# The first V weights issued between the first two x tiles instead of behind both, and one hoisted statistics instruction put back

## The chip, the cores and the metric

The kernel runs on one core of a Trainium2 chip. The time is device microseconds of one execution; the "span" of a profile is the same execution without its launch, some 1.8 us shorter.

## The reference, cut to what matters

```python
x = A_x                                             # 2048 x 1024, bf16
h  = x + A(layernorm(x), wqkv, wo)                  # 32 heads of 32, causal, window of 256 keys
h2 = h + B(layernorm(h), w1, w2)                    # silu, 3584 wide
# A:  qkv = x @ wqkv ; softmax(q k^T) v ; @ wo
```

Only the beginning is touched here: the layernorm of the first 512 rows of x (four tiles of 128 rows), and V = layernorm(x) @ wqkv[:, 2048:3072].

## The kernel before: the parts that matter

All loads shown go through the queue of the Sync engine (SP). Ahead of everything, eleven dummy matmuls keep TensorE busy, so that its clock, which is granted at half or full speed, is up when the real work comes. Each x tile is normalised (VectorE, with a square root on ScalarE), transposed on TensorE, copied back by ScalarE, and then used by "V groups" of eight matmuls each.

```python
load_x(0, 0)                       # 256 KB
load_x(0, 1)
load_wqkv(2 * D)                   # V weights, columns 0..511: 1 MB, rows of 1 KB
load_wqkv(2 * D + 512)             # V weights, columns 512..1023
load_x(0, 2)
load_x(0, 3)
for c0 in (0, D, 512, D + 512):    # Q and K weights
    load_wqkv(c0)
...
for i in range(11):                # warming matmuls, on zeros
    nc.tensor.matmul(sc[0][:, i % 2, :], lhsT=warm[:, 0, 0:P], rhs=warm[:, 0, :], start=True, stop=True)
...
def ln_first(xt, st, rs, j, stats=None, then=None):
    ln_stats(xt, st, j, stats)                       # two bn_stats and a bn_aggr on VectorE
    nc.scalar.activation(out=rs[:, j:j + 1], in_=st[:, j, 1:2], func=ACT.Sqrt, bias=eps[:], scale=1.0)
    if then is not None:
        nc.vector.bn_stats(out=then[0], in_=then[1])  # half of the next tile's statistics
    nc.vector.reciprocal(out=rs[:, j:j + 1], in_=rs[:, j:j + 1])
    for h in range(2):
        ln_norm(xt[:, h * 512:(h + 1) * 512], st, rs, j)
...
stats1 = small.tile([P, 2, 6], F32, name="ln_st", tag="ln_st")
ln_first(x_ring[0], st, rs, 0, then=(stats1[:, 0, :], x_ring[1][:, 0:512]))
turn_first(x_ring[0], lnT_b[0], 0)                   # 8 transposes on PE, 2 copies on ACT
ln_first(x_ring[1], st, rs, 1, stats=stats1)
v_group(0, 0, 0, act)                                # 8 matmuls, tile 0 x first V weights
turn_first(x_ring[1], lnT_b[0], 1)
ln_first(x_ring[2], st, rs, 2)
v_group(0, 1, 0, act)                                # tile 1: the "second V group" below
v_group(0, 0, 1, act)
...
```

The softmax here doesn't subtract the row's maximum and nothing guards it: scores larger than these inputs give would overflow.

Of the kernel before, what the change touches and what calls it, by code (L numbers as in the profile page):

```python
# [9 lines left out]
F32 = mybir.dt.float32  # L10
# [4 lines left out]
P = 128  # L15
# [21 lines left out]
def kernel(  # L37
# [10 lines left out]
    nc = tc.nc  # L48
# [3 lines left out]
    S, D = x2d.shape  # L52
# [12 lines left out]
    small = ctx.enter_context(tc.tile_pool(name="small", bufs=2))  # L65
# [22 lines left out]
    def view(region, off, *dims):  # L88
        n = 1
        for d in dims:  # L90
            n *= d
        ap = region[:, off:off + n]
        if len(dims) == 2:
            return ap.rearrange("p (a b) -> p a b", b=dims[1])
        if len(dims) == 3:
            return ap.rearrange("p (a b c) -> p a b c", b=dims[1], c=dims[2])
        return ap
# [5 lines left out]
    x_ring = [view(r_o, i * 1024, 1024) for i in range(8)]  # L103
# [22 lines left out]
    def load_x(b, j):  # L126
        nc.sync.dma_start(out=x_ring[(b % 2) * 4 + j], in_=x2d[(b * 4 + j) * P:(b * 4 + j + 1) * P, :])  # L127

    def load_wqkv(c0):
        dst = wqk[:, :, c0:c0 + 512] if c0 < 2 * D else wv[:, :, c0 - 2 * D:c0 - 2 * D + 512]  # L130
        nc.sync.dma_start(out=dst, in_=wqkv_v[:, :, c0:c0 + 512])

    load_x(0, 0)
    load_x(0, 1)
    load_wqkv(2 * D)
    load_wqkv(2 * D + 512)
    load_x(0, 2)
    load_x(0, 3)
# [13 lines left out]
        nc.tensor.matmul(sc[0][:, i % 2, :], lhsT=warm[:, 0, 0:P], rhs=warm[:, 0, :], start=True, stop=True)  # L152


    def ln_stats(xt, st, j, stats=None):
        first = 0
        if stats is None:
            stats = small.tile([P, 2, 6], F32, name="ln_st", tag="ln_st")
        else:
            first = 1  # L160
        for c in range(first, 2):
            nc.vector.bn_stats(out=stats[:, c, :], in_=xt[:, c * 512:(c + 1) * 512])
        nc.vector.bn_aggr(out=st[:, j, :], in_=stats[:])

# [17 lines left out]
    def ln_norm(xt, st, rs, j):  # L182
        nc.vector.tensor_scalar(out=xt, in0=xt, scalar1=st[:, j, 0:1], scalar2=rs[:, j:j + 1],
                                op0=ALU.subtract, op1=ALU.mult)
# [1 line left out]
    def ln_transpose(xt, dst, j):  # L186
        nc.sync.dma_start_transpose(out=dst[:, :, j * P:(j + 1) * P], in_=xt)

    def ln_first(xt, st, rs, j, stats=None, then=None):
        ln_stats(xt, st, j, stats)  # L190
        nc.scalar.activation(out=rs[:, j:j + 1], in_=st[:, j, 1:2], func=ACT.Sqrt, bias=eps[:], scale=1.0)
        if then is not None:
            nc.vector.bn_stats(out=then[0], in_=then[1])
        nc.vector.reciprocal(out=rs[:, j:j + 1], in_=rs[:, j:j + 1])
        for h in range(2):
            ln_norm(xt[:, h * 512:(h + 1) * 512], st, rs, j)

    def turn_first(xt, dst, j):
        for h in range(2):
            for i in range(4):  # L200
                kt = h * 4 + i
                nc.tensor.transpose(out=tp_ps[h][:, i * P:(i + 1) * P], in_=xt[:, kt * P:(kt + 1) * P], identity=ident[:])  # L202
            nc.scalar.copy(out=dst[:, h * 4:(h + 1) * 4, j * P:(j + 1) * P],  # L203
                           in_=tp_ps[h][:, 0:512].rearrange("p (k q) -> p k q", q=P))

    def ln_tiles(tag):
        st = small.tile([P, 4, 2], F32, name=f"st_{tag}", tag=f"st_{tag}")
        rs = small.tile([P, 4], F32, name=f"rs_{tag}", tag=f"rs_{tag}")
        return st, rs
# [9 lines left out]
    def v_group(b, j, c, copy):  # L219
        acc = next_acc()  # L220
        for kt in range(KT):
            nc.tensor.matmul(acc, lhsT=lnT_b[b % 2][:, kt, j * P:(j + 1) * P], rhs=wv[:, kt, c * 512:(c + 1) * 512],  # L222
                             start=(kt == 0), stop=(kt == KT - 1))
        copy(out=v[:, b * 4 + j, c * 16:(c + 1) * 16, 0:DH], in_=acc.rearrange("p (h d) -> p h d", d=DH))  # L224
# [108 lines left out]


    st, rs = ln_tiles("a")
    stats1 = small.tile([P, 2, 6], F32, name="ln_st", tag="ln_st")
    ln_first(x_ring[0], st, rs, 0, then=(stats1[:, 0, :], x_ring[1][:, 0:512]))
    turn_first(x_ring[0], lnT_b[0], 0)
    ln_first(x_ring[1], st, rs, 1, stats=stats1)
    v_group(0, 0, 0, act)  # L340
    turn_first(x_ring[1], lnT_b[0], 1)
    ln_first(x_ring[2], st, rs, 2)
    v_group(0, 1, 0, act)
    v_group(0, 0, 1, act)
# [13 lines left out]
    def ln1_steps(b):  # L358
        st, rs = ln_tiles("a")
        xs = [x_ring[(b % 2) * 4 + j] for j in range(4)]  # L360
        steps = [lambda j=j: ln_stats(xs[j], st, j) for j in range(4)]
        steps += rstd_steps(st, rs)
        for j in range(4):
            steps.append(lambda j=j: ln_norm(xs[j], st, rs, j))
        return steps, [lambda j=j: ln_transpose(xs[j], lnT_b[b % 2], j) for j in range(4)]

    def ln2_steps(b):
        st, rs = ln_tiles("b")
        hb = h_blk[b]
        load = lambda: nc.sync.dma_start(out=hb, in_=h_dram[b * 512:(b + 1) * 512, :].rearrange("(j p) d -> p j d", p=P))  # L370
        steps = [load]
        steps += [lambda j=j: ln_stats(hb[:, j, :], st, j) for j in range(4)]
        steps += rstd_steps(st, rs)
        for j in range(4):
            steps.append(lambda j=j: ln_norm(hb[:, j, :], st, rs, j))
        turns = [lambda j=j: ln_transpose(hb[:, j, :], ln2T[b], j) for j in range(4)]
        return steps[:-2] + [turns[0], steps[-2], turns[1], steps[-1]] + turns[2:]
# [104 lines left out]
    for b in range(NB):  # L482
# [4 lines left out]
        for ft in range(FT):  # L487
# [8 lines left out]
            if b == 0 and 6 <= ft < 14:  # L496
                j, c = divmod(ft - 6, 2)
# [60 lines left out]
```

## Time and profile before

| | |
|---|---|
| time, median of 3 runs | 701.58 us (699.18 to 703.16) |
| span of the profiled run | 700.0 us |
| TensorE busy | 688.5 us, 98% of the span |
| first V weights: issued, landed | 1.73 us, 9.44 us |
| first and second V group start | 9.48 us, 13.04 us |

TensorE is the bound throughout; only the first 13 us hold waits that a reordered load could shorten. The lines for this stand in the prediction. A row gives the stretch, its length, the busy time and number of instructions of TensorE (PE), weight loads, VectorE, ScalarE and GpSimd, then TensorE's granted clock, the busy share of the 16 DMA engines, and what they moved in GB/s.

```profile
4.00:5.50 1.50, 1.50 (x5) 0.58 (x4) 1.47 (x5) 0.29 (x1) 0.00 (x0) 1.00 0.89 298
7.60:11.03 3.43, 1.55 (x7) 0.76 (x8) 0.90 (x3) 0.56 (x2) 0.00 (x0) 0.96 1.08 363
11.03:14.44 3.41, 3.10 (x15) 1.47 (x14) 1.29 (x2) 1.56 (x3) 0.00 (x0) 0.54 1.09 356
```

Read the last three columns. In the later two stretches, and in the full ones below, the DMA share is about 1.08 (above 1 where packets of one engine overlap); between 4.0 and 5.5 us it is 0.89 and 298 GB/s, though much was queued. And the clock falls. The stretches are those of the prediction; at the edges that the clock records of this trace have, in steps of 3.41 us, the fall is sharp:

```profile
7.31:10.73 3.42, 1.25 (x6) 0.68 (x7) 0.90 (x3) 0.85 (x3) 0.00 (x0) 1.00 1.08 361
10.73:14.14 3.41, 3.10 (x14) 1.53 (x13) 1.00 (x2) 1.56 (x3) 0.00 (x0) 0.50 1.08 356
```

TensorE was busy 1.25 of 3.42 us, and then had half its clock from 10.73 to 14.14 us.

### The profile page before, as it was taken

To read this page: it belongs to the slowest core of one execution; us is meant where nothing else is said; L and a number is where in the kernel's file an instruction comes from. 1 tells how busy PE (TensorE), PEld (TensorE's weight loads), DVE (VectorE), ACT (ScalarE), POOL (GpSimd) and SP (SyncE) were. 2 spreads that over 40 slices of the span, in tenths; PEclk is the share of its full clock that TensorE was granted. 3 is DMA by queue.
4 is the path that set the end of the run, shared out by engine and by line. 5 is a ranking of instruction groups with operands and counts; after the bars stand their busy time and mean duration, and the time that the engine had idled before them with its cause. 6 is when DMAs were issued, how large, how long until landed. Compare 5 with 4: busy or idle time off the path is not lost.

```text
span 700.0 us, 12171 instructions
## 1 busy us (share of the span) xinstructions
PE 688.5 (98%) x4970; PEld 336.1 (48%) x5059; DVE 286.3 (41%) x608; ACT 259.7 (37%) x335; POOL 172.2 (25%) x375
## 2 busy tenths in 40 slices
PE   7999999999999999999999999999999999999998
PEld 3444555555555555544444444444444444444445
DVE  5356645754344347643324324434134351233111
ACT  3416567777777777621320023300033200233000
POOL 1005666777777777700000000000000000000000
PEclk9999999999999999999999999999999999999999
DMA  9532123024530678982023410023300034100110
GB/s 302 178 54 68 39 47 98 17 47 107 166 122 16 166 220 282 240 257 105 31 76 91 105 46 1 0 68 91 78 6 0 7 93 97 46 1 0 31 38 22
DMA packets 75399, 60.55 MB, mean 87 GB/s; under 512 B 49232, under 2 KB 59472, under 8 KB 75344
## 3 DMA queue, kind: packets, MB, share of 16 engines
q1 hardware_dynamic: 75344, 59.78, 30.3%
q8 instruction: 39, 0.64, 0.4%
q14 instruction: 16, 0.13, 0.1%
HBM read 39.85 MB, written 8.39 MB: 69 GB/s over the span
## 4 chain that ended last, share of the span: by engine, by line
PE 97%; DMA 1%; issue 1%; ACT 0%; SPq 0%; DVE 0%
PE hacc L468 18%; PE hacc L505 17%; PE acc L230 16%; PE acc L505 10%; PE acc L468 9%; PE acc L222 8%; PE acc L249 7%; PE o_ps L303 5%; PE sc L267 4%; PE hacc L249 1%; DMA r_w<-in_A_wqkv_dram 1%; PE o_ps L202 0%; SPq L127 0%; ACT r_a L224 0%; ACT r_w L203 0%
## 5 line engine op out<-in xcount | busy, mean ns | idle before, releaser
L278 ACT ACTIVATE r_e<-sc 128x1024 bf16<-128x1024 f32 (+2 forms) x192 | 175.8, 967 | 66.1 <-PE sc L267 52.5
L293 POOL TENSOR_SCALAR_AFFINE_SELECT r_e<-r_e 128x256 bf16<-128x256 bf16 (+1 forms) x368 | 169.3, 489 | 123.4 <-ACT r_e L278 120.3
L505 PEld LDWEIGHTS <-r_a 128*128 128x128 bf16 x952 | 90.9, 98 | 103.0
L468 PEld LDWEIGHTS <-r_w 128*128 128x128 bf16 x896 | 87.4, 98 | 104.8
L505 PE MATMUL hacc<-r_a 128*128 128x512 bf16 (+2 forms) x605 | 121.9, 359 | 0.6
L468 PE MATMUL hacc<-r_e,r_w 128*128 128x512 bf16 x444 | 100.2, 379 | 0.6
L477 ACT ACTIVATE r_n<-hacc 128x512 f32<-128x512 f32 x30 | 17.9, 597 | 178.9 <-PE hacc L468 178.9
L230 PEld LDWEIGHTS <-r_w 128*128 128x128 bf16 x512 | 46.1, 98 | 58.6 <-issue 8.9
L505 PE MATMUL acc<-r_a 128*128 128x512 bf16 x328 | 73.6, 379 | 0.4
L232 DVE CAST r_a<-acc 128x512 bf16<-128x512 f32 x56 | 38.7, 691 | 81.2 <-PE acc L230 57.7
L303 PEld LDWEIGHTS <-r_e 128*128 128x128 bf16 x1440 | 50.3, 96 | 22.7
L230 PE MATMUL acc<-r_t,r_w 128*128 128x512 bf16 x240 | 60.0, 380 | 0.8
L230 PE MATMUL acc<-r_w 128*128 128x512 bf16 x246 | 57.7, 380 | 0.5
L303 PE MATMUL o_ps<-r_a,r_e 128*128 128x33 bf16 x1440 | 51.2, 178 | 0.0
L249 PE MATMUL acc<-r_o,r_a 128*128 128x512 bf16 x196 | 48.7, 380 | 0.6
L468 PE MATMUL acc<-r_e,r_w 128*128 128x512 bf16 x216 | 49.1, 379 | 0.0
L249 PEld LDWEIGHTS <-r_a 128*128 128x128 bf16 x256 | 23.1, 98 | 29.6 <-issue 5.1
L267 PE MATMUL sc<-r_a 32*128 32x128 bf16 (+2 forms) x704 | 37.2, 276 | 0.0
L520 DVE SCALAR_TENSOR_TENSOR r_t<-hacc,r_t 128x512 bf16<-128x512 f32 (+2 forms) x22 | 14.0, 635 | 56.6 <-PE hacc L505 56.6
L520 DVE SCALAR_TENSOR_TENSOR r_t<-acc,r_t 128x512 bf16<-128x512 f32 x12 | 8.3, 692 | 64.2 <-PE acc L505 59.7
L478 DVE SCALAR_TENSOR_TENSOR r_a<-r_n,hacc 128x512 bf16<-128x512 f32 x30 | 20.6, 688 | 33.0 <-ACT r_n L477 33.0
L222 PE MATMUL acc<-r_w 128*128 128x512 bf16 x122 | 30.4, 390 | 2.8 <-DMA r_w<-in_A_wqkv_dram 2.2
(66 smaller groups left out, 425.7 us busy)
## 6 DMA issues: line engine op xcount, KB each, us to landing
r_w<-in_B_w_dram SPq DMA_DIRECT2D x8, 896.0 KB, 5.5
r_a<-in_B_w_dram SPq DMA_DIRECT2D x7, 1024.0 KB, 7.9
r_w<-in_A_wqkv_dram SPq DMA_DIRECT2D x6, 1024.0 KB, 11.2
r_o<-in_A_x_dram SPq DMA_DIRECT2D x16, 256.0 KB, 4.0
h_dram<-r_t SPq DMA_DIRECT2D x16, 256.0 KB, 3.2
r_t<-h_dram SPq DMA_DIRECT2D x16, 256.0 KB, 2.9
out_dram<-r_t SPq DMA_DIRECT2D x31, 128.0 KB, 1.7
r_e<-h_dram SPq DMA_DIRECT2D x3, 1024.0 KB, 5.7
```

The costliest lines, as they stand in the source:

```text
L222: nc.tensor.matmul(acc, lhsT=lnT_b[b % 2][:, kt, j * P:(j + 1) * P], rhs=wv[:, kt, c * 512:(c + 1) * 512], start=(kt == 0), stop=(kt == KT ...
L230: nc.tensor.matmul(acc, lhsT=wqk[:, kt, col0:col0 + P], rhs=lnT_b[b % 2][:, kt, :], start=(kt == 0), stop=(kt == KT - 1))
L232: copy(out=(qT, kT)[which][b][:, g, :], in_=acc)
L249: nc.tensor.matmul(acc, lhsT=qT[b][:, g, j * P:(j + 1) * P], rhs=wo[:, g, c * 512:(c + 1) * 512], start=(g == 0), stop=(g == G - 1))
L267: nc.tensor.matmul(sc[hh // 2][:, hh % 2, ch * P:(ch + nq) * P], lhsT=kT[t // 4][r0:r0 + DH, g, (t % 4) * P:(t % 4 + 1) * P], rhs=qT[b][r0 ...
L278: nc.scalar.activation(out=e[:, :, lo:hi], in_=sc[pair][:, :, lo:hi], func=ACT.Exp, scale=scale)
L293: nc.gpsimd.affine_select(out=ap, in_=ap, pattern=[[0, 2], [0, n], [sgn, P]], compare_op=ALU.is_ge if upper else ALU.is_gt, fill=0.0, base ...
L303: nc.tensor.matmul(o_ps[pair][:, qt * 2 + hh, 0:VW], lhsT=e_of(i, kind, pair)[:, hh, ch * P:(ch + 1) * P], rhs=v[:, b * 4 + kt, g * 4 + pa ...
L468: nc.tensor.matmul(acc, lhsT=w1[:, kt, ft * P:(ft + 1) * P], rhs=ln2T[b][:, kt, :], start=(kt == 0), stop=(kt == KT - 1))
L478: nc.vector.scalar_tensor_tensor(out=gT[:, ft, :], in0=th, scalar=1.0, in1=acc, op0=ALU.add, op1=ALU.mult)
L505: nc.tensor.matmul(acc[:, 0:c1 - c0], lhsT=gT[:, ft, j * P:(j + 1) * P], rhs=w2[ft // 4][:, ft % 4, c0:c1], start=(ft == 0), stop=(ft == F ...
L520: nc.vector.scalar_tensor_tensor(out=t_out[j % 2][:, c0:c1], in0=acc[:, 0:c1 - c0], scalar=0.5, in1=t_in[j % 2][:, c0:c1], op0=ALU.mult, o ...
```

## The change

Its intent, in its author's words: "so that large transfers follow the small one". The V weights go out behind tile 0 and ahead of tile 1. Since tile 1 then lands later, the half of its statistics that VectorE did early, in the middle of tile 0's LayerNorm, goes back to its own place.

```diff
     load_x(0, 0)
+    load_wqkv(2 * D)
     load_x(0, 1)
-    load_wqkv(2 * D)
     load_wqkv(2 * D + 512)
 ...
-    def ln_first(xt, st, rs, j, stats=None, then=None):
-        ln_stats(xt, st, j, stats)
+    def ln_first(xt, st, rs, j):
+        ln_stats(xt, st, j)
         nc.scalar.activation(out=rs[:, j:j + 1], in_=st[:, j, 1:2], func=ACT.Sqrt, bias=eps[:], scale=1.0)
-        if then is not None:
-            nc.vector.bn_stats(out=then[0], in_=then[1])
         nc.vector.reciprocal(out=rs[:, j:j + 1], in_=rs[:, j:j + 1])
 ...
-    stats1 = small.tile([P, 2, 6], F32, name="ln_st", tag="ln_st")
-    ln_first(x_ring[0], st, rs, 0, then=(stats1[:, 0, :], x_ring[1][:, 0:512]))
+    ln_first(x_ring[0], st, rs, 0)
     turn_first(x_ring[0], lnT_b[0], 0)
-    ln_first(x_ring[1], st, rs, 1, stats=stats1)
+    ln_first(x_ring[1], st, rs, 1)
```

More of the change, by code (lines that the diff above doesn't have):

```diff
@@ L152, with ln_stats @@
         nc.tensor.matmul(sc[0][:, i % 2, :], lhsT=warm[:, 0, 0:P], rhs=warm[:, 0, :], start=True, stop=True)
-    def ln_stats(xt, st, j, stats=None):
-        first = 0
-        if stats is None:
-            stats = small.tile([P, 2, 6], F32, name="ln_st", tag="ln_st")
-        else:
-            first = 1
-        for c in range(first, 2):
+    def ln_stats(xt, st, j):
+        stats = small.tile([P, 2, 6], F32, name="ln_st", tag="ln_st")
+        for c in range(2):
             nc.vector.bn_stats(out=stats[:, c, :], in_=xt[:, c * 512:(c + 1) * 512])
```

## The prediction

> **What bounds the kernel now.** I read the chain that ended last first, then the same chain for the first 40 us alone, then the timeline of the first 15 us, since the diff touches nothing later. The page's chain and its waits for TensorE:
>
> ```profile
> PE 97%; DMA 1%; issue 1%; ACT 0%; SPq 0%; DVE 0%
> ...
> L222 PE MATMUL acc<-r_w 128*128 128x512 bf16 x122 | 30.4, 390 | 2.8 <-DMA r_w<-in_A_wqkv_dram 2.2
> ```
>
> TensorE carries 97% of the 700.0 us span; the DMA share of 1% is one load of V weights. In the second line "x122" counts V matmuls, and the last field says that they waited 2.8 us in all, 2.2 of them for those weights. The chain cut to the first 40 us tells where:
>
> ```profile
> 1.73 7.71 DMA r_w<-in_A_wqkv_dram
> ...
> 9.48 2.40 PE acc L222 x8
> ...
> 11.91 0.59 ACT r_a L224
> 12.50 0.49 ACT r_w L203
> ...
> 13.04 3.72 PE acc L222 x14
> ```
>
> Columns are start, duration, what. The first V weights are issued at 1.73 and landed 7.71 us later, at 9.44; the first V group starts at 9.48. From 13.04 on TensorE has no wait to speak of: busy time by stretches gives it 13.40 of the 13.51 us up to 26.55, and 652.71 of the 660 us after 40. So a change in the start is worth what it does to the time 13.04, when the second V group begins, and no more. The timeline up to there:
>
> ```profile
> 3.47 1.29 DVE L162 BATCH_NORM_STATS2 ln_st<-r_o 128x6 f32<-128x512 bf16 x2 [1.97 <-DMA r_o<-in_A_x_dram]
> 4.91 0.64 DVE L193 BATCH_NORM_STATS2 ln_st<-r_o 128x6 f32<-128x512 bf16 x1
> 6.22 1.06 PE L202 MATMUL o_ps<-ident,r_o 128*128 128x128 bf16 x8
> 9.48 2.39 PE L222 MATMUL acc<-r_w 128*128 128x512 bf16 x8 [2.20 <-DMA r_w<-in_A_wqkv_dram]
> 11.67 1.06 PE L202 MATMUL o_ps<-ident,r_o 128*128 128x128 bf16 x8
> 13.14 1.29 DVE L162 BATCH_NORM_STATS2 ln_st<-r_o 128x6 f32<-128x512 bf16 x2 [4.01 <-DMA r_o<-in_A_x_dram]
> 15.23 0.73 DVE L183 TENSOR_SCALAR r_o<-r_o,st_a,rs_a 128x512 bf16<-128x512 bf16 x2
> ```
>
> Tile 0 lands at about 3.4 and is transposed from 6.22. Tile 1 (issued at 1.27, landing 2.8 us later, at about 4.1) has its LayerNorm finished near 9.1, so its transposes at 11.67 wait for nothing but the V group ahead of them. Tile 2 lands at 13.1; its transposes come only at 17.03, though its normalising began at 15.23: it is hidden.
>
> **What the Trainium skill says.** "DMA: Bandwidth & Descriptors", section "Queues, rings and completion order", says that the transfers of one issuing engine share one ring on each of 16 DMA engines and are consumed in ring order there, with no order between engines; its section "Why a DMA increments its semaphore by 16 and not by 1" says that only the full count means that all has landed. The trace agrees: between 1.5 and 9.5 us the queue moved 306 GB/s x 8.0 us = 2.45 MB, though tile 0, tile 1 and the first V weights are together only 0.26 + 0.26 + 1.05 = 1.57 MB. The other 0.88 MB are later transfers that quicker engines had begun; the landing is that of the slowest engine. The same page, section "Where 436 GB/s comes from", gives about 358 GB/s as a core's limit from HBM; this trace has 350 GB/s (6.2 to 9.5 us) and 365 (9.5 to 13), so the start is a full queue, and reordering trades one landing for another. "TensorE: Matmul & The Clock Gate", section "Part 1: The HAM clock gate", says that the clock halves or is restored by how busy TensorE was in a free-running window of 3.4 us. The trace agrees: granted clock 0.96 from 7.60 to 11.03 us, 0.54 from 11.03 to 14.44, 1.00 afterwards. In the first of these stretches TensorE was busy 1.55 us, and the clock then fell; in the second 3.10 us, and it rose.
>
> **The change part by part.**
>
> *Order of loads.* The V weights move from third to second place on the queue. They gain one issue slot, 1.73 - 1.27 = 0.46 us, and no longer have tile 1's 256 KB ahead of them, 0.26 MB at 350 GB/s = 0.75 us. The two are the same gain seen at two ends of the queue, not to be added. I choose 0.55 us: the first group starts at about 8.9 instead of 9.48. Tile 1 falls behind 1 MB. The bytes ahead of its end are those that were ahead of the end of the weights, so it lands about when the weights landed before, 9.4, or up to 0.3 us later where the queue has nothing ready between tile 0 and the many short rows of the weights (in before, the stretch 3.5 to 4.0 us moved only 156 GB/s although tile 1 was there to fill it). I take 9.6 us, against 4.1 before. Everything from the second V load on has the same bytes ahead of it, so tile 2 still lands near 13.1.
>
> *Removed hoist.* One bn_stats of 0.64 us no longer sits between the sqrt of tile 0 and its reciprocal; ScalarE's sqrt ended at 5.32, the reciprocal began at 5.47, so tile 0 is ready some 0.1 us sooner. TensorE then only waits longer for the weights: worth 0. The same bn_stats comes back in tile 1's own chain, which now begins on landing. DVE's instruction count and work stay the same; the order of the other engines doesn't change.
>
> *Tile 1's chain.* Tile 2 shows it without a hoist: statistics at 13.14, normalising at 15.23, its first half done 0.41 us later: 2.5 us from landing to the first transpose. Tile 1: 9.6 + 2.5 = 12.1 us. Meanwhile the first V group runs from 8.9 and takes the 2.19 us of before or a little less (down to eight times 0.22 = 1.75 us as more of it falls in the full-clock window): done at about 10.7. **TensorE then waits about 1.4 us for the LayerNorm of tile 1**, where it waited for nothing. Before, the first transpose at 11.67 led to the second V group at 13.04, 1.37 us, with ScalarE's copy of the V group in between; now ScalarE is free by then, so four transposes (0.45 us at the low clock), one copy of 0.59 and some 0.1 of hand-over: 1.15 us. Second V group: 12.1 + 1.15 = 13.25 against 13.04. **Sum: 0.2 us slower.**
>
> *Clock.* The wait is moved, and split: one idle stretch of 2.4 us (about 7.0 to 9.48) becomes 1.9 us (7.0 to 8.9) and 1.4 us (10.7 to 12.1). If the window from 11.03 to 14.44 is then busy only 2.1 of 3.4 us, it may not restore the clock. The only evidence: the warm-up was busy 2.65 us between 0.78 and 4.20 and its matmuls stayed at about 0.43 us each until 6.4. Another window at half clock costs about half of 3.4 us, 1.7 us. Against that, idle time in two pieces may keep the clock from dropping at all in some executions, which would save as much. I give the first 0.4 and the second 0.15: 0.25 x 1.7 = 0.4 us. So +0.2 + 0.4 = +0.6, less a little for the doubt that tile 1 lands as late: +0.4, 702.0 us.
>
> **Rivals.** (a) The intended gain: tile 1 rides along with the weights and lands early enough for its LayerNorm to be hidden behind the first V group. For it: that group starts 0.55 us sooner. Against it: 2.5 us of LayerNorm don't fit into 1.75 to 2.2 us of matmuls even when both land together. At its best (both land at 8.7, transposes at 11.2, second group at 12.35) it gains 0.7 us: 700.9. (b) The weights' landing is set by one lagging engine that isn't helped by the order; the first group stays at 9.5, tile 1 lands at 10 or later, its transposes start at 12.5 to 13: the second group at 13.7 to 14.2, with one more slow window 702.2 to 704.4. For it: the 0.88 MB moved ahead of the landing. (c) All is hidden and the clock phase, which is chance, decides: 701.6. None of the three comes near 2%, which is 14 us, and the whole stretch that the change can touch is 13 us long.
>
> **Range and chances.** The three runs of before span 4 us (699.18 to 703.16), more than any of these effects, so the range comes from that scatter: 702.0, with 699.8 to 704.2. Within 2%: 0.98; the rest is split evenly.
>
> **What would show it.** In the changed kernel: the first V group starts before 9.2 us and still waits for the weights; DVE's first statistics of tile 1 wait for DMA and start at 9.3 to 10; TensorE's transposes of tile 1 wait for DVE, some 1 to 2 us, which is a new wait; the second V group starts at 13.0 to 13.6; tile 2 lands within 0.5 us of 13.1; from there on the timelines agree, but for a possible second stretch at half clock. It is wrong if tile 1 lands together with the weights well before 9 us (then rival a), if the weights gain nothing (b), or if the time moves by more than 3 us, for then something after 40 us has changed that I take to be untouched.

## The result, and the profile after

| | before | after |
|---|---|---|
| median of 6 runs each | 701.61 us | 699.66 us |
| lowest to highest | 699.18 to 703.16 | 699.17 to 699.97 |
| span of the profiled run | 700.0 us | 697.4 us |

The ratio is 0.9972, with a 95% interval of 0.9954 to 0.9989: the same within 2%, and yet a gain clear of noise, of about 2 us. (The profiled run of the changed kernel, 699.17 us, was the fastest of its six, so the 2.6 us between the two spans is more than the typical gain.) It lies just outside the predicted range (699.8 to 704.2) and is a gain where a small loss was predicted. (A ratio here is the mean time of one kernel's fast runs over that of the other's of the same rounds, so not quite the ratio of the medians quoted.) Note the second row: the lowest time hardly moved; what went is the scatter upwards.

The chain that ended last, cut to the first 40 us, of the changed kernel (start, duration, what):

```profile
1.73 5.55 DMA r_o<-in_A_x_dram
...
7.30 1.30 DVE ln_st L158 x2
...
9.40 0.42 DVE r_o L179
...
9.87 0.41 PE o_ps L196 x4
...
10.30 0.59 ACT r_w L197
...
10.94 3.19 PE acc L216 x14
```

The chain's load is no longer the V weights but tile 1. It lands at 7.28, and its LayerNorm, transposes and copy lead to the second V group. The timeline of the same stretch:

```profile
3.70 1.29 DVE L158 BATCH_NORM_STATS2 ln_st<-r_o 128x6 f32<-128x512 bf16 x2 [2.20 <-DMA r_o<-in_A_x_dram]
7.30 1.29 DVE L158 BATCH_NORM_STATS2 ln_st<-r_o 128x6 f32<-128x512 bf16 x2 [0.78 <-DMA r_o<-in_A_x_dram]
7.33 1.90 PE L216 MATMUL acc<-r_w 128*128 128x512 bf16 x8 [0.36 <-ACT r_w L197]
9.87 0.72 PE L196 MATMUL o_ps<-ident,r_o 128*128 128x128 bf16 x8 [0.63 <-DVE r_o L179]
10.94 3.63 PE L216 MATMUL acc<-r_w 128*128 128x512 bf16 x15 [0.35 <-ACT r_w L197]
10.97 1.29 DVE L158 BATCH_NORM_STATS2 ln_st<-r_o 128x6 f32<-128x512 bf16 x2 [0.84 <-DMA r_o<-in_A_x_dram]
```

The first V group starts at 7.33 instead of 9.48, and what it waits for is ScalarE's copy of tile 0, not the weights, which landed at 1.27 + 5.3 = 6.6. Their issue, before and after (the last figure is us from issue to landing):

```profile
r_w<-in_A_wqkv_dram SPq DMA_DIRECT2D x1, 1024.0 KB, 7.7
r_w<-in_A_wqkv_dram SPq DMA_DIRECT2D x1, 1024.0 KB, 5.3
```

TensorE has a new wait of 0.63 us for tile 1's LayerNorm. Even tile 2, whose place in the queue didn't change, lands at 10.97 instead of 13.14. The second V group starts 13.04 - 10.94 = 2.10 us sooner. By stretches:

```profile
4.00:5.50 1.50, 1.50 (x6) 0.55 (x4) 1.19 (x3) 0.24 (x1) 0.00 (x0) 1.00 1.09 375
7.60:11.03 3.43, 2.44 (x17) 1.10 (x16) 2.15 (x7) 1.78 (x5) 0.00 (x0) 1.00 1.08 361
11.03:14.44 3.41, 3.36 (x16) 1.52 (x18) 2.98 (x8) 1.23 (x3) 0.00 (x0) 1.00 1.09 350
```

Two things differ, and both were in the profile before: the DMA queue is full from 4.0 us on (share 1.09, 375 GB/s), and the clock does not fall. The fall also slowed the second V group and its successors, up to 14.14 us: from the start of that group to the next transposes it is 3.99 us before (13.04 to 17.03) and 3.46 after (10.94 to 14.40), 0.53 us more. (That the first V group took 2.39 us instead of 1.90 is the clock's doing too, inside the 2.10.) 2.10 + 0.53 = 2.6 us, the whole difference between the spans; nothing after that changed.

### The profile page after: what moved, and what is told of

Its sections match the earlier page's. It is cut to its first block, busy times and chain, and to the rows that moved or that the text cites. A ratio compares the mean times of both kernels' runs of the same rounds, so it can differ in the third digit from the quotient of the medians.

```text
span 697.4 us, 12171 instructions
## 1 busy us (share of the span) xinstructions
PE 686.6 (98%) x4970; PEld 334.9 (48%) x5059; DVE 286.5 (41%) x608; ACT 259.9 (37%) x335; POOL 172.3 (25%) x375
## 4 chain that ended last, share of the span: by engine, by line
PE 97%; DMA 1%; issue 1%; DVE 0%; ACT 0%; SPq 0%
PE hacc L461 18%; PE hacc L498 17%; PE acc L224 16%; PE acc L498 10%; PE acc L461 9%; PE acc L216 8%; PE acc L243 7%; PE o_ps L297 5%; PE sc L261 4%; PE hacc L243 2%; DMA r_o<-in_A_x_dram 1%; PE o_ps L196 0%; DVE ln_st L158 0%; ACT r_w L197 0%; DVE r_o L179 0%
## 5 line engine op out<-in xcount | busy, mean ns | idle before, releaser
L224 PE MATMUL acc<-r_w 128*128 128x512 bf16 x246 | 57.7, 380 | 0.5
L461 PE MATMUL hacc<-r_a,r_w 128*128 128x512 bf16 x141 | 32.7, 379 | 0.2
```

The costliest lines, as they stand in the source:

```text
L224: nc.tensor.matmul(acc, lhsT=wqk[:, kt, col0:col0 + P], rhs=lnT_b[b % 2][:, kt, :], start=(kt == 0), stop=(kt == KT - 1))
L461: nc.tensor.matmul(acc, lhsT=w1[:, kt, ft * P:(ft + 1) * P], rhs=ln2T[b][:, kt, :], start=(kt == 0), stop=(kt == KT - 1))
```

## The experiments

My theory after seeing the result, **S**: in the old order some DMA engines start on the V weights late, so the weights land late; and TensorE's longer idle time then lets the clock fall. The rivals: it was the chance of one execution; it was the hoist; the clock alone; the late weights alone. (The profile shows the mean busy share of the 16 DMA engines, not how many work; where an expectation counts engines, I judge by the rate.)

### 1. The kernel before again

No edit.

> The kernel before, unchanged, timed against itself and profiled a second time. Theory S (the old order of loads makes some DMA engines start the first V weights late, each time): again only 9 to 14 of 16 engines at work between 4.0 and 5.5 us, a rate of 170 to 310 GB/s there, the first V group at 9 to 9.7 us, and run times scattered over some 3 us or more. Rival N (the lag was the chance of one execution): the first V group at 7.5 to 8.5 us in this profile, rate above 340 GB/s from 4.0 us.

Measured: median 701.48 us (699.73 to 702.96), 1.0003 of before, interval 0.9980 to 1.0026. TensorE's timeline:

```profile
8.53 3.45 PE L222 MATMUL acc<-r_w 128*128 128x512 bf16 x8 [1.77 <-DMA r_w<-in_A_wqkv_dram]
13.15 3.63 PE L222 MATMUL acc<-r_w 128*128 128x512 bf16 x15 [0.60 <-ACT r_w L203]
```

The weights landed at 8.5, about 0.9 us earlier than in the first profile, so the lateness varies; the rate between 4.0 and 5.5 us was 356 GB/s, above what S had expected; the gap lay earlier (share 0.92, 287 GB/s from 3.3 to 4.4 us). But the eight matmuls took 3.45 us instead of some 1.9, since the clock had fallen already (0.66 granted from 7.60 to 11.03), and the second group is as late as ever. Neither expectation fits wholly: rival N's 8.5 us holds, S's late second group too. So the cost of lateness isn't fixed by the landing alone: the clock goes into it.

### 2. The new order alone, hoist kept

```diff
# against the kernel before
     load_x(0, 0)
+    load_wqkv(2 * D)
     load_x(0, 1)
-    load_wqkv(2 * D)
```

> The kernel before with the new order of loads alone, the hoisted statistics kept. Theory S: the weights land near 6.4 as in the changed kernel, but VectorE, which works in order, now stops at the hoisted statistics until tile 1 lands at about 7.3, with the reciprocal of tile 0 behind it: tile 0's transposes at about 8.4 instead of 6.3, the first V group near 9.5, the second near 11.7 (tile 1's chain is then short of one statistics, and its transposes follow the V group at once): time between the two kernels, about 700.5. Rival (the hoist does not matter): same as the changed kernel, 699.7.

Measured: median 703.05 us, 1.0028 of before (1.0007 to 1.0048): slower. VectorE's and TensorE's timelines:

```profile
7.36 0.70 DVE L193 BATCH_NORM_STATS2 ln_st<-r_o 128x6 f32<-128x512 bf16 x1 [2.18 <-DMA r_o<-in_A_x_dram]
8.62 0.72 PE L202 MATMUL o_ps<-ident,r_o 128*128 128x128 bf16 x8 [2.19 <-DVE r_o L183]
```

The weights were there at 1.26 + 5.3 = 6.6, where S said 6.4. But VectorE took its instructions in order: the hoisted statistics of tile 1 stopped it for 2.18 us until that tile landed, with tile 0's reciprocal behind them, and TensorE waits 2.19 us for tile 0. The second V group starts at 14.14, later than the 11.7 that I expected: the clock fell again, so the first V group took 3.28 us instead of 1.90, and I had left too little for the way from the first transpose of tile 1 (12.77) to that group. So the two parts of the diff belong together: the order makes the hoist harmful.

### 3. The hoist alone removed, old order

```diff
# against the changed kernel
     load_x(0, 0)
-    load_wqkv(2 * D)
     load_x(0, 1)
+    load_wqkv(2 * D)
```

> The changed kernel with the old order of loads, so the hoist alone removed from the kernel before. Theory S: time as before, 701.6, the first V group at 9 to 9.7 us, weights late. Rival H (the hoist's removal is what gained): 699.7.

Measured: median 700.79 us, 1.0004 of before (0.9977 to 1.0031). The hoist's removal by itself is worth nothing that shows. In the profile the weights landed at 8.2, the first V group took 3.46 us at half clock, and the second began at 12.92: the picture of experiment 1. (S had expected a first V group at 9 to 9.7; it came at 8.30, so the weights were less late than that.) The median falls between the two expected; the ratio decides for S.

### 4. Weights late, clock held

```diff
# against the kernel before
     turn_first(x_ring[0], lnT_b[0], 0)
+    for i in range(9):
+        nc.tensor.matmul(sc[0][:, i % 2, :], lhsT=warm[:, 0, 0:P], rhs=warm[:, 0, :], start=True, stop=True)
```

> The kernel before with nine more dummy matmuls between the transposes of tile 0 and the first V group, where TensorE waits for the weights. They keep the clock up and shorten nothing. If the fall of the clock between 11.0 and 14.4 us is a good part of the loss, the clock stays at 1.00 after 7.6 us and the time falls by 1.3 to 1.8 us to about 700.1. If the late weights alone are the loss, the time stays at 701.6.

Measured: median 700.69 us (699.80 to 701.86), ratio 0.9994 (0.9973 to 1.0015): too close to tell by time. The profile tells:

```profile
6.77 2.11 PE L340 MATMUL sc<-r_e 128*128 128x512 bf16 x9
9.29 1.89 PE L222 MATMUL acc<-r_w 128*128 128x512 bf16 x8 [0.41 <-DMA r_w<-in_A_wqkv_dram]
12.34 3.63 PE L222 MATMUL acc<-r_w 128*128 128x512 bf16 x15 [0.72 <-ACT r_w L203]
```

The weights were late (9.2), the clock stayed at 1.00, the V group took 1.89 us, and the span is 699.0 us: 1.0 below the profile of before, 1.6 above that of the changed kernel. The mean granted clock was 0.999 or 1.000 in all six runs. So with the clock held, late weights still cost time, and holding it is worth somewhat under 1 us between these two profiles (the weights landed 0.2 us sooner here). In an execution where the weights come early the nine matmuls would stand in the way until 8.9, so it is no cure.

### 5. The changed kernel again

No edit.

> The changed kernel again, beside the others: 699.2 to 700.0 in every run, granted clock 1.000 in every run, weights landed before 7.3, second V group at 10.8 to 11.1. If its good first series was luck of the clock's phase: some runs at 0.998 and 701 to 702.

Measured: median 699.37 us (699.09 to 700.17), 0.9977 of before (0.9956 to 0.9997), granted clock 1.000 in five runs and 0.999 in one. Weights landed at 1.26 + 5.6 = 6.9, second V group at 11.20 (expected: up to 11.1; two runs, 699.09 and 700.17, lie just outside the expected 699.2 to 700.0). The first series was no luck.

### 6. What the fast runs of the kernel before are

The kernel before had runs of 699.2 us too. Four looks, to catch one in a trace.

> The kernel before, one look. If the old order makes DMA engines late only in some executions: a run below 700.0 us has its first V group at 7.3 to 7.8 and its second at 10.8 to 11.4, with all 16 DMA engines at work from 4.2 us; a run above 701 has 8.2 or later and 12.3 or later. If the clock alone parts them: a run below 700.0 has weights at 8.2 to 9.4 too, and a granted clock of 1.00 after 7.6 us.

> The kernel before, a second look, with the same two expectations: below 700.0 us, either weights landed by 7.8 (late engines only in some executions) or weights late and the clock at 1.00 throughout.

> The kernel before, a third look, with the same two expectations: below 700.0 us, either weights landed by 7.8 (late engines only in some executions) or weights late and the clock at 1.00 throughout.

> The kernel before, a fourth look, with the same two expectations: below 700.0 us, either weights landed by 7.8 (late engines only in some executions) or weights late and the clock at 1.00 throughout.

Measured: 702.28, 699.41, 703.63 and 702.65 us. The second look caught one. TensorE's timeline of look 2, then of look 3:

```profile
8.13 1.89 PE L222 MATMUL acc<-r_w 128*128 128x512 bf16 x8 [0.96 <-DMA r_w<-in_A_wqkv_dram]
11.19 3.63 PE L222 MATMUL acc<-r_w 128*128 128x512 bf16 x15 [0.72 <-ACT r_w L203]
```

```profile
10.14 3.57 PE L222 MATMUL acc<-r_w 128*128 128x512 bf16 x8 [2.96 <-DMA r_w<-in_A_wqkv_dram]
14.88 3.92 PE L222 MATMUL acc<-r_w 128*128 128x512 bf16 x15 [0.31 <-ACT r_w L203]
```

Profiles of the kernel before, and the two of the changed kernel, by their landings. "Landed" is issue plus time to landing of the first V weights; the clock is the mean granted in the two stretches. (The traces of "after again" and look 2 hold no clock record at all, and the profile then gives 1.00; that their clock was up is borne out by their V groups, 1.90 and 1.89 us.)

| run | landed | clock 7.60-11.03 / 11.03-14.44 | second V group | span |
|---|---|---|---|---|
| after | 6.6 | 1.00 / 1.00 | 10.94 | 697.4 |
| after again | 6.9 | 1.00 / 1.00 | 11.20 | 697.9 |
| before, look 2 | 8.1 | 1.00 / 1.00 | 11.19 | 697.6 |
| before again | 8.5 | 0.66 / 0.84 | 13.15 | 699.7 |
| before | 9.4 | 0.96 / 0.54 | 13.04 | 700.0 |
| before, look 3 | 10.1 | 0.66 / 0.50 | 14.88 | 701.8 |

(Looks 1 and 4 landed at 9.6 and 9.9, with spans of 700.5 and 700.9.) The span is the start of the second V group plus 686.4 to 687.0 us in every row: all differences but the 0.5 us of a clock still low behind that start arise before it. The earliest landing of the old order, 8.1, costs 0.2 us against the first profile of the changed kernel and nothing against the second. A landing 0.4 us later with a fall of the clock costs 2.1 us (699.7 against 697.6), of which at least 1.7 are the clock. A landing at 10.1 with a longer fall costs 4.2. Of my two expectations for look 2 the second is nearly met: its weights came at 8.1 (not by 7.8, where the other had them), and its clock held. So weights that land by 8.1 cost next to nothing, as the new order has its own wait for tile 1; what they cost beyond that shows between look 2 and experiment 4, both at full clock: landing 1.1 us later (9.2), second V group 1.15 later. A fall of the clock comes on top.

When does it fall? I put stretches of 3.41 us at the edges of each trace's clock records. In fifteen profiles, of all kernels here, the records reach back far enough. In nine of them the first stretch after the recorded rise has TensorE busy 0.29 to 1.67 us, and the clock then falls; in six it is busy 1.81 to 3.18 us, and no fall follows. The edges lie differently in each execution (the first recorded rise is at 4.68 to 7.31 us in the old order), so the same idle time can lead to a fall or not. In the two profiles of the changed kernel no stretch of 3.41 us that begins between 4 and 12 us (tried in steps of 0.2 us) is busy less than 2.42 us, and in look 2 none less than 2.33; in the first profile of before the least is 1.21. So, judged by these figures, no position of the edges would have brought a fall with early weights; with late ones it is chance.

The times of the timed runs agree. On two chips, 29 runs of the kernel before, by their mean granted clock: 14 at 1.000, 699.20 to 701.27 us, mean 699.9; 11 at 0.997 or 0.998, 701.32 to 703.08; 4 at 0.995, 702.96 to 703.71. (A mean of 1.000 is no proof of full speed from the start, see experiment 7.)

### 7. The clock alone, in the new order

```diff
# against the changed kernel
-    for i in range(11):
+    for i in range(6):
```

> The changed kernel with 6 instead of 11 warming matmuls: TensorE idles from 4.1 to 6.3 us, the loads are untouched. If the clock is a large part of what the late weights cost: the clock rises later in most executions, the first V group runs at half speed, weights and tile 1 landing as before, median 1 to 2 us above the changed kernel (700.7 to 701.7) and scattered. If the clock matters little: 699.4 to 699.8.

Measured: median 700.10 us (699.15 to 700.67), 0.9984 of before (0.9964 to 1.0004), on a chip where the changed kernel itself was not timed. TensorE's timeline:

```profile
7.67 3.60 PE L216 MATMUL acc<-r_w 128*128 128x512 bf16 x8 [0.25 <-ACT r_w L197]
12.43 3.63 PE L216 MATMUL acc<-r_w 128*128 128x512 bf16 x16 [0.31 <-ACT r_w L197]
```

The first V group is on time (7.67) but takes 3.60 us instead of 1.90; the second starts at 12.43 and the span is 698.9 us, 1.5 above the profile of the changed kernel. That is the price of the clock with the loads left alone, in this execution. The median is below the 700.7 to 701.7 that I expected; how many of its runs escaped the low clock can't be told, since the granted clock of the profiled run is 1.00 too: its first clock record is at 12.27 us, and what lies before counts as full speed.

### 8. What makes the weights late

Four orders in which the transfers ahead of the weights differ. The table gives the rate from 4.0 to 5.5 us and when the first V weights landed; the old order itself had 229 to 376 GB/s and 8.1 to 10.1 us in eight profiles, the new order 362 to 376 GB/s and 6.6 to 6.9 us in four.

```diff
# e4_merged, against the changed kernel: tiles 0 and 1 in one transfer of 512 KB
+    nc.sync.dma_start(out=r_o[:, 0:2048].rearrange("p (j d) -> p j d", d=D),
+                      in_=x2d[0:2 * P, :].rearrange("(j p) d -> p j d", p=P))
     load_wqkv(2 * D)
# e6_actq: tiles 0 and 1 as before, the first V weights issued by ScalarE
+    load_wqkv(2 * D, nc.scalar)
# e9_rows2k: old order, V weights by halves of the contraction, rows of 2 KB
+    nc.sync.dma_start(out=wv[:, 0:4, :], in_=wqkv_v[:, 0:4, 2 * D:3 * D])
+    nc.sync.dma_start(out=wv[:, 4:8, :], in_=wqkv_v[:, 4:8, 2 * D:3 * D])
# e10_three: tiles 0, 1 and 2 ahead of both halves of the V weights
+    load_x(0, 1)
+    load_x(0, 2)
     load_wqkv(2 * D)
```

> Tiles 0 and 1 as one transfer of 512 KB ahead of the first V weights: the bytes ahead of the weights as in the kernel before, the number of transfers ahead (one) as in the changed kernel. Theory B (the amount of short work ahead of the weights makes engines start them late): lag as before, 9 to 14 engines at work around 4 to 5 us, times scattered over 3 us with a median near 701.5. Theory T (a second transfer between the first and the weights does it): all 16 at work from about 4 us, weights landed by 7.3, times within 1 us; tile 0 lands some 0.6 us later, so the first V group at 7.9 to 8.2, and tile 1 is early, so the second at about 11: 699.7.

> The old order, but the first V weights are issued from ScalarE's queue, so their descriptors need not come behind those of the two tiles. If the lag is one of descriptors that come late behind two other transfers of the same queue: weights and tiles begin together near 2.2 us, all 16 engines at work throughout, weights landed by 7, tiles 0 and 1 some 0.5 us later than before; first V group 7.3 to 8, time 699.2 to 700, scatter within 1 us. If the lag is in the DMA engines themselves: 9 to 14 at work around 4 to 5 us and times scattered as before.

> Old order, the V weights loaded by halves of the contraction (rows of 2 KB, half as many rows for the same bytes); the first V group then needs both megabytes and the time must be worse, some 703; it is run for the DMA alone. If engines idle because rows are described too slowly behind two short transfers (supply of descriptors): the rate from 4.0 to 5.5 us rises from 298 GB/s (first profile of the kernel before) to 350 or more. If two short transfers ahead of a long one do it whatever the rows: 300 to 340 GB/s again.

> Tiles 0, 1 and 2, all three ahead of the first V weights. If short work ahead makes the lag: it grows, the weights land at 9.5 to 11 us, second V group 13 to 15, median 702 to 704. If it is that descriptors come too late: the third tile gives 0.75 us more time to write them, all engines at work from 4.5 us on, weights landed at 8.0 to 8.5, median 700 to 701.

| ahead of the weights | GB/s, 4.0-5.5 us | landed | time |
|---|---|---|---|
| one transfer of 512 KB | 378 | 7.8 | median 700.48; 3 runs at 699.6, 3 at 701.3 to 701.6 |
| two tiles, weights from ScalarE's queue | 389 | 8.2 | median 700.01 (699.84 to 700.42) |
| two tiles, rows of 2 KB (first half) | 239 | 9.9 | one look, 704.57 |
| three tiles | 190 | 10.6 | median 702.75 (700.20 to 703.64) |

```profile
4.00:5.50 1.50, 1.50 (x5) 0.59 (x4) 0.70 (x2) 0.00 (x0) 0.00 (x0) 1.00 1.06 378
```

```profile
4.00:5.50 1.50, 1.50 (x5) 0.59 (x4) 1.16 (x3) 0.27 (x1) 0.00 (x0) 1.00 0.85 239
```

The first row above is the merged kernel, the second the one with rows of 2 KB. The rate in this one stretch is not a sure mark: three of the eight profiles of the old order had 348 to 376 GB/s there and yet landed at 8.1 to 8.5, their gap lying before 4 us (231 to 299 GB/s from 3.5 to 4.0). A better one is what had been moved when the weights landed (mean rate times landing) beyond what had to be:

```profile
0.00:9.44 9.44, 5.73 (x19) 2.48 (x20) 5.11 (x14) 2.84 (x5) 2.97 (x7) 1.00 0.78 257
0.00:6.58 6.58, 4.57 (x15) 1.66 (x16) 2.94 (x8) 1.58 (x2) 2.97 (x7) 1.00 0.70 240
0.00:7.78 7.78, 5.08 (x17) 1.81 (x18) 3.09 (x9) 1.58 (x2) 2.97 (x7) 1.00 0.72 243
```

Before: 2.43 MB, 0.86 more than the 1.57 needed; changed: 1.58 MB, 0.27 more than the 1.31 needed; merged: 1.89 MB, 0.32 more than 1.57. All eight of the old order have 0.48 to 0.91 MB too much, all four of the new order 0.27 to 0.32. So with the same 512 KB ahead of the weights the lag is as small as in the new order when they are one transfer, and larger when they are two. Halving the number of rows per byte does not help (0.97 MB too much; against the theory that rows are described too slowly); the third tile does not help either (0.83 MB; the weights landed at 10.6, where 8.0 to 8.5 was expected if they merely needed more time). Issued from ScalarE's queue, the weights leave the DMA busy, but this run answers less than it was meant to: they came at 8.2 and tile 1 at 7.2, neither by 7 nor only 0.5 us later, which fits two queues that share the engines.

What is shown, by one profile of each of these orders, is that the lateness goes with two or more short transfers ahead of a long one in the same queue, not with their bytes and not with the number of rows. Why some DMA engines then fall behind is not settled. The merged kernel met its theory T only in part: weights at 7.8 instead of 7.3, second V group at 11.51 instead of 11, and times 2 us apart instead of 1. It shows the clock again: tile 0 now waits for both tiles (its statistics start at 4.80), TensorE idles 1.15 us for it, and half its runs have a granted clock of 0.998 and 1.8 us more.

### 9. Two tries at the new wait

The changed kernel waits 0.63 us for tile 1's LayerNorm. Two ways to bring the tile sooner:

```diff
# e5_split, against the changed kernel
     load_x(0, 0)
-    load_wqkv(2 * D)
+    nc.sync.dma_start(out=wv[:, 0:4, 0:512], in_=wqkv_v[:, 0:4, 2 * D:2 * D + 512])
     load_x(0, 1)
+    nc.sync.dma_start(out=wv[:, 4:8, 0:512], in_=wqkv_v[:, 4:8, 2 * D:2 * D + 512])
# e8_x1_act, against the changed kernel: tile 1 issued by ScalarE, at the same time as tile 0 by SP
+    load_x(0, 1, nc.scalar)
     load_x(0, 0)
     load_wqkv(2 * D)
```

> The changed kernel with the first V weights in two halves of 512 KB, tile 1 between them. If the new wait of TensorE for tile 1's LayerNorm (0.6 us at 9.87 in the changed kernel) is what now bounds the start: tile 1 lands near 5.8 instead of 7.3, its transposes follow the V group at 9.1 to 9.3, the second V group starts at 10.3 instead of 10.94, time 0.6 us below the changed kernel, about 699.0. Rival: the further switch between transfers brings the lag back, the first V group waits for the second half at 8 to 9.5, times scattered, 700 or more.

> The changed kernel with tile 1 issued from ScalarE's queue, at the same time as tile 0 from the Sync queue; the V weights stay second on the Sync queue. If TensorE's wait for tile 1's LayerNorm (0.5 to 0.6 us) is what is left to gain: tile 1 lands near 4, its transposes follow the first V group at once, second V group at 10.3 to 10.5, 699.0 in every run. Rival: with two short transfers ahead of the weights again, some engines start the weights late, the first V group at 8 or later, times scattered, median 700 or more.

Measured: split, median 700.09 us (699.65 to 701.16), 0.9989 of before; tile 1 from ScalarE, 701.22 us (700.57 to 702.05), 1.0003. Both rivals had the times right, the second not the reason. In the split kernel the rate was 304 GB/s from 4.0 to 5.5 us and tile 1 landed only at 7.0, 0.3 us earlier than unsplit; tile 2 came at 12.32. With tile 1 from the other queue the weights were not held up (384 GB/s from 4.0 to 5.5 us, landed at 1.26 + 6.5 = 7.8, 0.30 MB moved too much, with two tiles ahead but in two queues). But the two tiles came together, tile 1 at 4.7 and tile 0 at 4.9, and tile 0, which everything waits for, was late (VectorE's timeline):

```profile
4.95 1.28 DVE L158 BATCH_NORM_STATS2 ln_st<-r_o 128x6 f32<-128x512 bf16 x2 [3.46 <-DMA r_o<-in_A_x_dram]
```

That is 1.25 us behind the 3.70 of the changed kernel, more than the 0.63 us to be won. The changed kernel has the lowest median of all that ran, though not all on one chip.

## Why the prediction was wrong, point by point

**"The weights' landing is that of the slowest engine": right as an observation, wrongly used.** The 0.88 MB moved beyond what was needed were the sign of engines that lag behind others. I took the lag as given, and computed the new landings from those of before: "I choose 0.55 us", the first group at 8.9, and tile 1 "about when the weights landed before", 9.6 us. This is the step that failed. With little lag, tile 0, tile 1 and the weights have all landed by 7.3 us in the new order (the weights at 6.6, tile 1 at 7.28); in the old order it took 0.8 to 2.8 us longer for the same 1.57 MB. The lag belonged to the order that the change removes. Hence also "tile 2 still lands near 13.1" (10.97) and the first group's wait for the weights (there was none). The reading behind it, "so the start is a full queue", holds from 5.5 us on: from 3.5 to 4.0 us the trace had 156 GB/s, from 4.0 to 5.5 us 298, and the new order moved 375 there. A check was at hand: 1.57 MB at 350 GB/s are 4.5 us, and almost nothing moves in the first 2 us (19 GB/s), so by this estimate 6.5 us; measured, 7.3, not 9.4.

**"TensorE then waits about 1.4 us for the LayerNorm of tile 1": right mechanism, size off.** The wait is there, 0.63 us. The 2.5 us from landing to transpose that I took from tile 2 is right: 7.28 to 9.87 is 2.6. The wait is shorter because the V group starts at 7.33, just when tile 1 lands, and so covers most of its LayerNorm; the prediction had the group start 0.7 us before that landing.

**"Second V group: 13.25": measured 10.94.** The last leg, 1.15 us from transpose to V group, is 1.07.

**"Removed hoist: worth 0": right alone** (experiment 3), but it is what makes the new order usable (experiment 2, 3.7 us slower than the changed kernel on the same chip by the medians), which the prediction did not say.

**The clock: the right suspect, the wrong sign.** I gave 0.4 to another window at half clock and 0.15 to none. In the 12 runs of the changed kernel the mean granted clock was never below 0.999, while it was 0.998 or less in 15 of 29 of the kernel before. With V weights by 6.9 us TensorE's longest wait after the warming matmuls is 0.63 us in place of 2.20, and no fall followed. This followed from the wrong landing. (The stretch of 1.55 busy us that the prediction read was not the one the clock goes by; that was 7.31 to 10.73, with 1.25. Its idle stretch of 2.4 us is 2.20 by the line that it shows. Its worry that a stretch busy 2.1 us might not restore the clock was sound: in look 3 and in the kernel with rows of 2 KB the clock stayed at half after stretches busy 1.95 and 2.26 us.)

**Rival (a)** named the intended gain and bounded it at 0.7 us, with both landings at 8.7: the same error. **"The range comes from that scatter"** failed as a rule too: the scatter of the kernel before was not noise about a mean but a mixture of executions with more and less lateness, with and without a fallen clock, and the change takes away the bad ones.

**Right:** within 2%; nothing after the start changes; tile 1's statistics wait for DMA and its transposes for VectorE.

## What to carry to other kernels

When a transfer lands much later than its bytes explain, ask whether the lateness belongs to the order of the queue before carrying it over into a changed order; compute the landing from bytes and rate as well. At a cold start, try one short transfer ahead of the long one rather than two (it paid here), and see what an in-order engine that reads the postponed tile would now hold up. A scatter of run times that goes with the granted clock is a cost that can be taken away: count executions by clock before calling it noise, and look at the durations of the matmuls as well, since the mean granted clock can miss the start.

## What the Trainium skill lacked or had wrong

- "DMA: Bandwidth & Descriptors", section "Queues, rings and completion order", tells that a later transfer can complete before an earlier one, but not that short transfers ahead of a long one on the same queue can hold the long one up: 8.1 to 10.1 us to land and 0.48 to 0.91 MB moved beyond need in the eight profiles of the old order, against 6.6 to 6.9 us and 0.27 to 0.32 MB in the four with one short transfer ahead.
- The same page, section "Issuing engines are not separate DMA queues", says that transfers from several engines interleave, which the trace bears out, and that this only saves the sequencer's time. Here it also changed what lands first: with tile 1 on ScalarE's queue, tile 0 landed at 4.9 instead of 3.7 us; with the weights there, tile 1 landed at 7.2 instead of 4.1 us.
- "TensorE: Matmul & The Clock Gate", section "Part 1: The HAM clock gate", gives an idle window as the condition of the low clock in its table of states. A partly busy one was enough: TensorE was busy 1.25 of 3.42 us from 7.31 to 10.73, and the clock was then 0.50. Of the fifteen profiles of experiment 6, a fall followed 0.29 to 1.67 busy us in nine, and none followed 1.81 to 3.18 in six.
- No page that I read says that the mean granted clock of a profile takes the time before its first clock record as full speed: in experiment 7 the profile gives 1.00 for 7.60 to 11.03 us, where eight matmuls took 3.60 us instead of 1.90.
